# Sixteen small transfers in an earlier slot, one issuing queue, low parts on GpSimd, and three batches in another order

## The chip, the cores and the metric

The kernel runs on one core of a Trainium2 chip. The metric is the device time of one execution in microseconds (us); lower is better. Five engines work side by side: TensorE (PE) multiplies, VectorE (DVE), ScalarE (ACT) and GpSimd (POOL) do the rest, and SyncE (SP) only issues transfers (DMAs). ACT issues some transfers too, and does nothing else while one of its issues is held back.

## The reference

Two small attentions are computed between `x` and a state of 32 vectors per head, their results are put behind one another (512 + 32 tokens for each of 8 batches, 512 wide), and a gated two-layer network is applied to all 4608 tokens.

```python
B, H, S, Ns, D = (8, 8, 512, 32, 64)
a = softmax(x @ state.T / 8);   xread = a @ state
a2 = softmax(state @ x.T / 8);  sread = a2 @ x
t = concatenate([xread, sread], axis=2).transpose(0, 2, 1, 3).reshape(B * 544, H * D)
h = t @ w_in                    # 512 x 2048
g = h * tanh(softplus(h))       # mish
out = g @ w_out                 # 2048 x 512
```

The 256 `sread` tokens are called the read vectors below.

## The kernel before

Every fp32 product is made of three products of rounded parts (hi by hi, hi by lo, lo by hi); ACT makes a high part by a cast, DVE the low part by a subtraction (`ah`/`al`, `gh`/`gl`, `swh`/`swl`, `srT`).

The work goes batch by batch. For `xread` the kernel never forms the 512 tokens: it multiplies the state by `w_in` (`swp`, needing slices of `w_in` that are loaded again from memory, `w_in_again`), and then the softmax `a` by that product (`ph`). ACT turns `ph` by Mish into a unit `u`; POOL sums parts of units (`sums`), ACT and DVE split them (`gh`, `gl`), and PE multiplies them with `w_out` and sums of it into four accumulators (`acc_one`, `acc_two`, `acc_top`, `acc_end`: seven products in place of eight). At the end of a half batch ACT and DVE add the accumulators up (`sums<-acc_one` and so on) before PE may start the next half in the same banks.

Beside it the next batches are prepared. `e2_turned` (steps `tu`, `TU`; line 392) transposes the second softmax on DVE (`u<-e`), and 16 DMAs (line 404) put the 32-row quarters in place (`e2T`), which PE multiplies with `x` into `srp`; DVE scales that to the read vectors `srds`. `soft1_a` (step `PR`) makes `ah` and `al` of the next batch.

The read vectors of all batches go through the network at the end of batch 6 and in batch 7 (`ph_s`). For this those of batches 0 to 5 are transposed on DVE (`sr_turned`) and moved by 16 DMAs on SP (`sr_moved`, line 548; step `rm`), and split into `srT` high and low parts (step `rs`); those of batches 6 and 7 are turned on PE (`srTp`, step `rt`).

The order on each engine is written out by hand: a string of steps for batch 0 (line 873 on) and a `TABLE` for batches 1 to 7 (line 1061 on), one row for each of 8 slots (a slot multiplies one 256-wide piece of `w_in`). `G`, `M` are the projection and its Mish; `A`, `B` multiply a unit with `w_out`, `P`, `p` prepare one; `wN` loads a slice of `w_in` again; `lx`, `ly` load `x`. Each engine keeps this order strictly (class `InOrder`), so an instruction that waits holds all that follows it there. The DMAs of SP and ACT take eight completion semaphores in turn, and each is issued only when the transfer eight back, whichever of the two engines issued it, has landed.

Batch 7's `x` and four of its 16 `e2T` DMAs are issued by ACT:

```python
(nc.scalar if b in (1, B - 1) and 4 * q + c < 4 else nc.sync).dma_start(
    both[quad(q), c].rearrange("p k t n -> p (k t n)"), u[quad(c), q].rearrange("i k m -> i (k m)"))
```

Of the kernel before, what the change touches and what calls it, by code (L numbers as in the profile page):

```python
# [9 lines left out]
F32 = mybir.dt.float32  # L10
# [7 lines left out]
P = 128  # L18
B, H, S, NS, D = 8, 8, 512, 32, 64
# [3 lines left out]
NT = S // P  # L23
# [11 lines left out]
def as_f32(ap):  # L35
    return ap.bitcast(F32)
# [16 lines left out]
def quad(q):  # L53
    return slice(q * NS, (q + 1) * NS)
# [27 lines left out]
def state_attention_mish_kernel(ctx, tc, x, state, w_in, w_out, out):  # L82

    nc = tc.nc
    pe, dve, act, pool_e = (InOrder(tc, e) for e in (nc.tensor, nc.vector, nc.scalar, nc.gpsimd))
# [3 lines left out]
    pool = ctx.enter_context(tc.tile_pool(name="pool", bufs=2))  # L89
# [36 lines left out]
    def load_x(b, xs=None, by=nc.sync):  # L126

        shape = [P, NC, 2, NT * D]
        if xs is not None:
            pass  # L130
        elif b == 0:
            xs = const.tile(shape, F32, tag="wo7", name="x_0")
        else:
            tag, bufs = ("x", 1) if b == 2 else ("raw", 2)
            xs = pool.tile(shape, F32, tag=tag, name=f"x_{b}", bufs=bufs)
        for c in range(NC):
            last["load"] = by.dma_start(
                xs[c] if isinstance(xs, list) else xs[:, c],
                x[b].rearrange("(c k) (p t) d -> c p k (t d)", k=2, t=NT)[c])
        return xs  # L140
# [127 lines left out]
    xss = {0: load_x(0)}  # L268
# [7 lines left out]
    def attention(b, sn, x_in=None):  # L276
        sc, e2T, srd, aT = {}, {}, {}, {}
# [114 lines left out]
        def e2_turned():  # L392

            both = pool.tile([P, NC, 2, NT, NS], F32, tag="e2T", name=f"e2T_{b}", bufs=1)
            for kc in range(2):
                e2T[kc] = both[:, :, kc]
            u = pool.tile([P, 4, 2, NT * NS], F32, tag={0: "u0", 2: "sw2"}.get(b, "sc"), name=f"u_{b}", bufs=1)
            for kc in range(2):
                dve.transpose(
                    u[:, :, kc].rearrange("i q (t n) -> i t q n", t=NT),  # L400
                    e2s[kc].rearrange("n (t q p) -> n t q p", t=NT, q=4))
            for c in range(NC):
                for q in range(4):
                    (nc.scalar if b in (1, B - 1) and 4 * q + c < 4 else nc.sync).dma_start(  # L404
                        both[quad(q), c].rearrange("p k t n -> p (k t n)"), u[quad(c), q].rearrange("i k m -> i (k m)"))

        two = range(2)
# [121 lines left out]

    srds = {}  # L530

    def srT_parts(bs, c, values):
        hi, lo = (srT[c // 2][:, :, i, bs.start * NS:bs.stop * NS].rearrange("p c (b n) -> p c b n", n=NS) for i in range(2))
        act.copy(hi, values)
        dve.tensor_sub(lo, values, as_f32(hi))

    early = range(B - 2)

# [14 lines left out]
    def sreads_split():  # L553
        for c, tag in ((0, "sc"), (2, "e2T")):
            srT.append(pool.tile([P, 2, 2, B * NS], F32R, tag=tag, name=f"srT_{c}", bufs=1))
            srT_parts(early, c, srds["moved"][:, c:c + 2])

    def sread_transposed():
        pt = misc("srTp")[:, :2 * P].rearrange("p (b c n) -> p b c n", b=2, n=NS)
# [98 lines left out]
    def s_item(j, r, k):  # L658


        fc = 2 * r + k
        w = wis[B - 1, j][:, :, fc * P:(fc + 1) * P]
        if (j, r, k) == (0, 0, 1):
            both = pool.tile([P, 2, NC, P], F32R, tag="wt", name="w_0_0_1", bufs=1)
            hi, lo = both[:, 0], both[:, 1]
        else:
            hi, lo = (pool.tile([P, NC, P], F32R, tag="t", name=f"w{n}_{j}_{r}_{k}", bufs=5) for n in "hl")
        act.copy(hi, w)
        dve.tensor_sub(lo, w, as_f32(hi))
        yield  # L670
        ph = (misc, first_bank)[k](f"ph_s_{j}_{r}_{k}")
        for c in range(NC):
            pe.matmul(
                ph, hi[:, c], srT[c // 2][:, c % 2].rearrange("p i t -> p (i t)"), start=(c == 0), stop=(c == NC - 1))
        for c in range(NC):
            pe.matmul(
                ph[:, :256], lo[:, c], srT[c // 2][:, c % 2, 0], start=False, stop=(c == NC - 1), skip_group_check=True)
        yield
        unit = made["s", 0, 2 * j + r] if k else new_unit("s", 0, 2 * j + r)
        to = unit[:, 1 - k].rearrange("f h t -> f (h t)")  # L680
        act.copy(to, ph[:, 256:])
        dve.tensor_add(to, to, ph[:, :256])
        yield
        last["mish"] = act.activation(to, to, AF.Mish)
# [188 lines left out]
    for step in """  # L873
            st st st x0 x1 ldi0 x2 x3 sc hia0 ldi1 acc sc sc sc hib0 sc dia0 tr0 tr0 tr1 tr0 ldo0 tr1 jia0 cib0
            tr1 st ex0 ex1 jib0 no fill6 sw0 cib1 cia1 no coa0 ldi2 sw0 fill2 ldo1 pr0 pr0 hia1 ldi4 pr1 ldi3
            dob0 pr0 hib1 pr1 sw0 hoa0 qa0 qb0 ldo2 ldi5 jia1 jib1 di2 hob0 hi2 fill2 pr1 sw1 sw1 qb1 qa1 ji2
            ldo3 fill2 sw1 ma0 joa0 mb0 job0 ko1 ma0 mb0 wha0 sw2 p1 lx co1 loa0 sw2 la0 ci3 m1 ldo4 whb0 ga0
            lb0 sw2 lob0 ko1 ldo5 ga0 ga0 ja1 ga0 gb0 hi3 ho2 m1 ji3 gb0 gb0 lg1 ja1 gb0 p2 ci4 co2 ldo6 ldi6
            lo1 do3 sw3 g1 jo2 sw3 hi4 ji4 jo2 sw3 lo2 n2 g1 n2 X1 ho3 lg2 ldi7 g1 X2 jo3 p3 mm1 hi5 ho4 m3 sw4
            di5 g1 X3 sw4 jo3 g2 ji5 co4 sw4 g2 m3 ho5 lo3 jo4 lg3 ST X0 g2 jo4 g2 co5 hi6 di6 sw5 p4 sw5 n4 lo4  # L880
            sw5 n4 XD0 ja5 ci7 g3 g3 ja5 g3 lg4 p5 ji6 m5 g3 g4 mm0 ee0 SC SC lo5 hi7 ee1 xi2 g4 sw6 m5 g4 lg5
            ldo7 sw6 SC TR1 g4 ji7 sw7 ho6 ee0 sw6 p6 ho7 co6 ee1 TR0 g5 TR1 g5 TR0 EX1 tu EX0 ja6 sw7 n6 co7 g5
            n6 NO xz0 sw7 ja6 g5 NO PR0 xy0 next lg6 lo6 p7 PR0 PR1 g6 g6 n7 PR0 PR1 next g6 sr0 sr1 ja7 PR1 n7
            sr0 g6 sr1 next ja7 lg7 lo7
            """.split():
        what, i = re.fullmatch(r"([a-zA-Z]+)(\d*)", step).groups()
        if not hasattr(begun.get(step), "send"):
            begun[step] = steps[what](int(i or 0))
        if hasattr(begun[step], "send"):
            next(begun[step], None)  # L890

    A12, A22, A11, A21 = range(4)
    S1, S3, S2, S4 = range(3, 7)
    T3, T4, T2 = range(3)
# [57 lines left out]
    def sevens(key, p):  # L952
        return {2: FIRST, 3: FIRST + 1 + p}.get(key, SEVEN)
# [38 lines left out]

    def sums_of(key, p, banks):

        tag, bufs = ("g", 6) if (key, p) == (B - 2, 0) else ("wt", 1)
        e = banks["sums"] = pool.tile([P, 4, 256], F32, tag=tag, name=f"sums_{key}_{p}", bufs=bufs)
        one, two = (banks[n].rearrange("t (h e) -> t h e", h=2) for n in ("one", "two"))
        act.copy(e[:, 0], one[:, 0])
        dve.tensor_sub(e[:, 3], e[:, 0], one[:, 1])
        dve.tensor_add(e[:, 1:3], two, e[:, 3:].to_broadcast([P, 2, 256]))  # L1000
        if sevens(key, p) < SLOTS:
            dve.tensor_add(e[:, 3], e[:, 1], two[:, 1])
        else:
            dve.scalar_tensor_tensor(e[:, 3], e[:, 1], -1.0, two[:, 1], ALU.mult, ALU.subtract)
# [48 lines left out]
    def half_slot(key, j, at):  # L1053
# [4 lines left out]
        elif ready and (ready[0][:2] != (key, 0) or ready[0][2] < j + (j == SLOTS - 1 and at)):  # L1058
# [1 line left out]

    TABLE = {
        1: """
            G0 M0 G1 M1 mm0 mm1 ee0 ee1 A h l X0 X1 ee0 ee1 X2 X3 XD tu w0
            G0 M0 G1 M1 S2 S2 h S2 B l ST w1
            G0 M0 G1 M1 h A B l
            G0 M0 G1 M1 h A SC sr0 sr1 S4 S6 SC sr0 sr1 S4 S4 S6 S6 lx B l MM0 MM1 T0
            G0 M0 G1 M1 h T0 A TR0 TR1 w2 B l T0 TR0 TR1 T1
            G0 M0 G1 M1 EE0 EE1 EX0 EX1 T1 h A w3 B l T1 NO EE0 EE1 T2 NO
            G0 M0 G1 M1 h A PR0 PR1 B l
            G0 M0 G1 M1 h PR0 PR1 A N0 PR0 PR1 N0 N0 T2 B l li""",  # L1070
        2: """
            G0 M0 G1 M1 X0 X1 X2 X3 T2 A T3
            G0 M0 G1 M1 S2 S2 S2 T3 XD B ST T3 A T4
            G0 M0 G1 M1 T4 w4 P p B P p T4 T4 tu
            P G0 M0 p G1 M1 P p A S4 SC S4 S4 SC w5 P p B MM0 MM1""",
        3: """
            P G0 M0 p G1 M1 P p X0 X1 A P X2 X3 p B
            P G0 M0 p G1 M1 S2 P p S2 S2 XD A ST P p B
# [22 lines left out]
        B - 2: """  # L1101
            P G0 M0 p G1 M1 P p X0 X1 A P X2 X3 p B
            P G0 M0 p G1 M1 S2 P p S2 S2 XD A ST P p B
            P G0 M0 p G1 M1 P p w4 A P p B
            P G0 M0 p G1 M1 P p A S4 SC S4 S4 SC lx w5 P p B MM0 MM1
            P G0 M0 p G1 M1 rm P p TR0 TR1 A P rm TR0 TR1 p B
            P G0 M0 p G1 M1 S6 sr0 sr1 P p S6 S6 sr0 sr1 w2 ly EE0 EE1 EX0 EX1 A EE0 EE1 P p TU B NO
            P G0 M0 p G1 M1 P p NO PR0 PR1 A P p B
            P G0 M0 p G1 M1 N0 PR0 PR1 P p N0 N0 PR0 PR1 A P p SR0 SR1 SR0 SR1 w3 rs B U rt W0 A W1 P p""",
        B - 1: """  # L1110
            P G0 M0 p G1 M1 P p A P p w4 B
            P G0 M0 p G1 M1 S2 P p S2 S2 w5 A P p B
# [14 lines left out]
    for key in [*range(1, B - 1), "s", B - 1]:  # L1127
        if key == "s":
            for i, item in enumerate(items):
                j, r, k = i // 4, i // 2 % 2, i % 2  # L1130
# [29 lines left out]
            xss[b] = load_x(b)  # L1160

        def load_last():
            xss[B - 1] = load_x(B - 1, by=nc.scalar)

        def load_next():
            global_next = key + 2
# [36 lines left out]
        for j, line in enumerate(steps_of(key)):  # L1203
# [11 lines left out]
            for step in line:  # L1215
                what, i = re.fullmatch(r"([a-zA-Z]+)(\d*)", step).groups()
                name = step if what == "T" else (key, step)
# [34 lines left out]
```

## Time and profile before

| | |
|---|---|
| median of 3 runs | 648.79 us (648.32 to 651.68) |
| the profiled execution | 649.55 us, of which the span from first to last instruction is 647.7 |
| PE busy | 628.2 us, 97% of the span |
| DVE, ACT, POOL busy | 441.3, 354.6, 197.9 us |
| mean granted TensorE clock | 0.991 of full speed |

PE is idle for 647.7 - 628.2 = 19.5 us in all. Its busy time also holds stretches at a lower granted clock, in which the same matmuls take longer. In a row of a timeline the number in brackets is the time for which the engine stood idle just before it, with what ended that; "ACTq" and "SPq" rows are issues of DMAs.

### The profile page before, as it was taken

Reading aid. Unit: us, or ns where it says so; the run is one execution under the profiler, and the core shown is the slowest. Engines: PE = TensorE matmul, PEld = TensorE weight load, DVE = VectorE, ACT = ScalarE, POOL = GpSimd, SP = SyncE. Lnnn points to the kernel's source line nnn. Section 1 sums busy time; section 2 is a strip of 40 time slices with the busy share of each in tenths; the row PEclk is TensorE's granted clock in tenths of the full one; section 3 lists DMA queues with packets and bytes.
Section 4 is the critical chain, followed back from the end, with each engine's and each line's share of the span. In section 5 each row is a group of like instructions: output and inputs, shape, how many; then the busy total and the mean of one; then the engine's idle time right before and its main releaser. Section 6 shows DMA issues by size and latency. Waiting matters only on the chain.

```text
span 647.7 us, 13630 instructions
## 1 busy us (share of the span) xinstructions
PE 628.2 (97%) x5379; PEld 536.2 (83%) x5379; DVE 441.3 (68%) x757; ACT 354.6 (55%) x720; POOL 197.9 (31%) x307
## 2 busy tenths in 40 slices
PE   8999999999999999999999999999996899999997
PEld 5776777787787887888888899888885799989897
DVE  5998965548676856887697856686582876635264
ACT  4998765455455534645456644654552566544442
POOL 0000000032432232304531663256321543443274
PEclk9999999999999999999999999999998899999999
DMA  8999904701446254614454455435524324320000
GB/s 323 410 323 326 333 28 116 229 23 50 123 124 202 66 151 129 195 50 131 116 171 124 125 143 164 132 77 148 163 93 134 98 66 131 99 66 16 19 33 32
DMA packets 71711, 88.77 MB, mean 137 GB/s; under 512 B 13792, under 2 KB 48608, under 8 KB 71648
## 3 DMA queue, kind: packets, MB, share of 16 engines
q1 hardware_dynamic: 69744, 86.40, 42.6%
q10 hardware_dynamic: 1904, 1.51, 0.8%
q8 instruction: 42, 0.69, 0.5%
q14 instruction: 21, 0.17, 0.1%
HBM read 62.85 MB, written 13.11 MB: 117 GB/s over the span
## 4 chain that ended last, share of the span: by engine, by line
PE 76%; DVE 8%; DMA 7%; ACT 4%; SPq 2%; issue 1%; POOL 0%; DVEq 0%; ACTq 0%
PE ph L74 22%; PE acc_top L74 10%; PE acc L74 10%; PE acc_one L74 8%; PE acc_two L74 8%; PE acc_end L74 6%; PE swp L74 4%; DMA wir<-in_moe_w_in_dram 3%; PE ph_s L74 3%; DVE gl L74 2%; SPq L404 2%; DMA e2T<-u 1%; PE srp L74 1%; PE acc_s_one L74 1%; DMA w_in<-w_in_again 1%
## 5 line engine op out<-in xcount | busy, mean ns | idle before, releaser
L74 POOL TENSOR_TENSOR sums<-u 128x256 f32<-128x256 f32 x87 | 68.7, 789 | 249.4 <-DVE gl L74 156.7
L74 ACT ACTIVATE u<-ph 128x256 f32<-128x256 f32 x192 | 63.2, 382 | 85.1 <-PE ph L74 81.8
L74 POOL TENSOR_TENSOR sums<-sums,u 128x128 f32<-128x128 f32 x174 | 101.6, 584 | 13.7
L74 DVE TENSOR_TENSOR gl<-u,gh 128x384 fp32r<-128x384 f32 (+1 forms) x96 | 58.4, 609 | 56.1 <-ACT gh L74 55.3
L74 DVE TENSOR_TENSOR gl<-sums,gh 128x512 fp32r<-128x512 f32 x87 | 66.2, 761 | 29.5 <-ACT gh L74 29.5
L74 PE MATMUL acc<-wo,gh 128*128 128x512 f32 x256 | 80.1, 394 | 0.0
L74 PE MATMUL ph<-ah,swh 128*128 128x512 f32 (+1 forms) x228 | 71.6, 396 | 7.4 <-ACT u L74 5.9
L74 PE MATMUL acc_top<-wo,gh 128*128 128x256 f32 (+1 forms) x384 | 78.0, 295 | 0.0
L74 ACT CAST gh<-u 128x384 fp32r<-128x384 f32 x87 | 44.7, 514 | 54.7 <-PE acc_end L74 32.8
L74 PE MATMUL ph<-al,swh 128*128 128x512 f32 (+1 forms) x228 | 71.1, 393 | 0.2 <-DVE al L74 0.2
L74 PE MATMUL ph<-ah,swl 128*128 128x512 f32 (+1 forms) x228 | 71.0, 392 | 0.1
L74 ACT CAST gh<-sums 128x512 fp32r<-128x512 f32 x87 | 54.1, 621 | 25.0 <-POOL sums L74 24.7
L74 PEld LDWEIGHTS acc_top<-wo,gh 128*128 128x128 f32 x384 | 61.0, 193 | 2.7 <-issue 0.8
L74 POOL TENSOR_TENSOR w_sums<-w_sums 128x256 f32<-128x256 f32 x16 | 13.0, 812 | 155.9 <-DVE w_sums L74 147.2
L74 PEld LDWEIGHTS acc<-wo,gh 128*128 128x128 f32 x256 | 47.4, 188 | 13.0 <-issue 3.3
L74 PE MATMUL acc_top<-wo,gl 128*128 128x256 f32 (+1 forms) x192 | 56.3, 293 | 0.0
L74 DVE TENSOR_TENSOR swl<-swp,swh 128x512 fp32r<-128x512 f32 (+1 forms) x60 | 36.4, 647 | 25.3 <-ACT swh L74 25.3
L74 PEld LDWEIGHTS ph<-ah,swh 128*128 128x128 f32 x228 | 40.2, 191 | 15.5 <-ACT u L74 6.1
L74 PEld LDWEIGHTS ph<-al,swh 128*128 128x128 f32 x228 | 43.1, 190 | 10.5 <-DVE al L74 1.2
L74 PEld LDWEIGHTS ph<-ah,swl 128*128 128x128 f32 x228 | 43.2, 190 | 9.9 <-DVE swl L74 0.7
L74 PE MATMUL acc<-wo,gl 128*128 128x512 f32 x128 | 49.9, 390 | 0.0
L74 ACT CAST swh<-swp 128x512 fp32r<-128x512 f32 (+1 forms) x60 | 30.5, 562 | 23.2 <-PE swp L74 23.2
(232 smaller groups left out, 1400.3 us busy)
## 6 DMA issues: line engine op xcount, KB each, us to landing
w_in<-w_in_again SPq DMA_DIRECT2D x27, 1024.0 KB, 5.9
wir<-in_moe_w_in_dram SPq DMA_DIRECT2D x16, 512.0 KB, 10.2
wor<-in_moe_w_out_dram SPq DMA_DIRECT2D x16, 512.0 KB, 9.5
x<-in_x_dram SPq DMA_DIRECT2D x28, 256.0 KB, 4.0
x_rows<-x_turned SPq DMA_DIRECT2D x56, 128.0 KB, 2.4
x_in<-in_x_dram SPq DMA_DIRECT2D x24, 256.0 KB, 3.1
out_dram<-sums SPq DMA_DIRECT2D x23, 256.0 KB, 5.2
w_in_again<-w_in_sb SPq DMA_DIRECT2D x4, 1024.0 KB, 9.5
```

Of the source, the lines that this page charges most:

```text
L74: made = method(*args, **kwargs)
L404: (nc.scalar if b in (1, B - 1) and 4 * q + c < 4 else nc.sync).dma_start(both[quad(q), c].rearrange("p k t n -> p (k t n)"), u[quad(c), q ...
```

## The change

It has five parts. (1) In batch 6 the step `rm` (two transposes, 16 DMAs) moves from slot 4 to slot 2 (slots are counted from 0). (2) Batch 7's `x` and all its `e2T` DMAs are issued by SP, `x` ahead of the `w_in` load of step `w2`. Its `u` transposes move ahead of the preparation of a unit. (3) The low parts of `srT` of batches 0 to 5 are made by POOL. (4) In batch 6 `al` is made after the first read vectors' weights, `sums_(5,1)` takes a buffer of `g` (`sr_moved` now holds the one it had), and one `ph_s` takes another PSUM bank. (5) In batch 2 the `e2T` step moves a slot back, behind two `w_in` loads; in batch 1 the transfers and `e2T` move a slot back, behind the `sw_1_2` parts, with `u` in another buffer and `sr`, `lx` a slot later; in batch 0 the steps `hi6 di6` (which scale a piece of `w_in` as it comes in) move behind a Mish, which makes the ACT tables change twice more.

```diff
-            u = pool.tile([P, 4, 2, NT * NS], F32, tag={0: "u0", 2: "sw2"}.get(b, "sc"), name=f"u_{b}", bufs=1)
+            u = pool.tile([P, 4, 2, NT * NS], F32, tag={0: "u0", 1: "wt", 2: "sw2"}.get(b, "sc"), name=f"u_{b}", bufs=1)
...
-                    (nc.scalar if b in (1, B - 1) and 4 * q + c < 4 else nc.sync).dma_start(
+                    (nc.scalar if b == 1 and 4 * q + c < 4 else nc.sync).dma_start(
...
-    def srT_parts(bs, c, values):
+    def srT_parts(bs, c, values, by=dve):
...
-        dve.tensor_sub(lo, values, as_f32(hi))
+        by.tensor_sub(lo, values, as_f32(hi))
...
-            srT_parts(early, c, srds["moved"][:, c:c + 2])
+            srT_parts(early, c, srds["moved"][:, c:c + 2], pool_e)
...
-        ph = (misc, first_bank)[k](f"ph_s_{j}_{r}_{k}")
+        ph = (misc, misc if (j, r) == (3, 1) else first_bank)[k](f"ph_s_{j}_{r}_{k}")
...
-        tag, bufs = ("g", 6) if (key, p) == (B - 2, 0) else ("wt", 1)
+        tag, bufs = ("g", 6) if (key, p) in ((B - 3, 1), (B - 2, 0)) else ("wt", 1)
...
-            P G0 M0 p G1 M1 P p w4 A P p B
+            P G0 M0 p G1 M1 P p w4 rm A P p rm B
...
-            xss[B - 1] = load_x(B - 1, by=nc.scalar)
+            xss[B - 1] = load_x(B - 1)
```

On SP, in batch 6, this is the order of the issues before (`w_in_5508` is the load of step `w4`, `w_in_5919` that of `w2`, `x_5649` batch 6's own next `x`):

```order
L572 DMA w_in_5508<-w_in_again 128x4x512
L137 DMA x_5649<-in_x_dram 128x2x256 x4
L572 DMA w_in_5654<-w_in_again 128x4x512
L692 DMA out_dram<-sums_1_5678 128x2x256 x2
L548 DMA sr_moved<-sr_turned_5740 32x192 x8
L548 DMA sr_moved<-sr_turned_5792 32x192 x8
L572 DMA w_in_5919<-w_in_again 128x4x512
L404 DMA e2T_5971<-u_5972 32x256 x12
L572 DMA w_in_6213<-w_in_again 128x4x512
```

And this is the same stretch of SP after the change, with the same loads under new numbers:

```order
L572 DMA w_in_5508<-w_in_again 128x4x512
L548 DMA sr_moved<-sr_turned_5511 32x192 x8
L548 DMA sr_moved<-sr_turned_5552 32x192 x8
L137 DMA x_5670<-in_x_dram 128x2x256 x4
L572 DMA w_in_5675<-w_in_again 128x4x512
L692 DMA out_dram<-sums_1_5699 128x2x256 x2
L137 DMA x_5919<-in_x_dram 128x2x256 x4
L572 DMA w_in_5924<-w_in_again 128x4x512
L404 DMA e2T_5961<-u_5962 32x256 x16
L572 DMA w_in_6211<-w_in_again 128x4x512
```

The 16 `sr_moved` issues left the place between the output and the `w_in` load, and batch 7's `x` and four more `e2T` stand there or right behind.

On ACT, at the end of batch 6's slot 5 and the start of slot 6, this stood before (`u_0_6`, `u_1_6` are the two units of slot 6):

```order
L74 CAST gh_0_5_5961<-sums_0_5_5963 128x512
L137 DMA x_5921<-in_x_dram 128x2x256 x4
L404 DMA e2T_5971<-u_5972 32x256 x4
L74 ACT_TABLE_LOAD
L74 ACTIVATE u_0_6_6025<-ph_6_0_6018 128x256
L74 ACTIVATE u_1_6_6027<-ph_6_0_6018 128x256
```

And this stands there now:

```order
L74 CAST gh_0_5_5981<-sums_0_5_5983 128x512
L74 ACT_TABLE_LOAD
L74 ACTIVATE u_0_6_6025<-ph_6_0_6018 128x256
L74 ACTIVATE u_1_6_6027<-ph_6_0_6018 128x256
L74 ACTIVATE u_0_6_6025<-ph_6_1_6029 128x256
```

No issue of a DMA is left between the cast and the table load.

On DVE, at the end of the first half of batch 6's output (slot 7), this stood before (`sums_6233` adds up the accumulators of that half):

```order
L74 TENSOR_TENSOR al_6135<-at_0_6050,ah_6134 128x512
L74 TENSOR_TENSOR al_6135<-at_1_6052,ah_6134 128x512
L74 TENSOR_TENSOR gl_1_0_6169<-u_1_0_5276,gh_1_0_6168 128x384
L74 TENSOR_TENSOR gl_1_0_6169<-sums_1_0_6170,gh_1_0_6168 128x512
L74 TENSOR_SCALAR srds<-srp_6178,rs_0_5956 128x64
L74 TENSOR_SCALAR srds<-srp_6178,rs_1_5959 128x64
L74 TENSOR_TENSOR srT_6215<-sr_moved,srT_6215 128x2x192
L74 TENSOR_TENSOR srT_6218<-sr_moved,srT_6218 128x2x192
L74 TENSOR_TENSOR sums_6233<-sums_6233,acc_0_one 128x256
```

And this stands there now, down to the two `al` rows:

```order
L74 TENSOR_TENSOR gl_1_0_6167<-u_1_0_5276,gh_1_0_6166 128x384
L74 TENSOR_TENSOR gl_1_0_6167<-sums_1_0_6168,gh_1_0_6166 128x512
L74 TENSOR_SCALAR srds<-srp_6176,rs_0_5956 128x64
L74 TENSOR_SCALAR srds<-srp_6176,rs_1_5959 128x64
L74 TENSOR_TENSOR sums_6231<-sums_6231,acc_0_one 128x256
L74 TENSOR_TENSOR sums_6231<-acc_0_two,sums_6231 128x512
L74 SCALAR_TENSOR_TENSOR sums_6231<-sums_6231,acc_0_two 128x256
L74 TENSOR_TENSOR sums_6231<-acc_0_top,sums_6231 128x2x256
L74 TENSOR_TENSOR sums_6231<-acc_0_end,sums_6231 128x256
L74 TENSOR_TENSOR srT_6213<-srTp,srT_6213 128x2x64
L74 TENSOR_TENSOR srT_6216<-srTp,srT_6216 128x2x64
L74 TENSOR_TENSOR wl_0_0_6266<-w_in_5924,wh_0_0_6265 128x512
```

Four DVE instructions left the way to `sums`: two went to POOL, and the two `al` now follow behind `wl_0_0`.

## Rows read from the trace of the kernel before

**Rows 1.** Window: length, busy PE, PEld, DVE, ACT, POOL, granted clock, DMA share, GB/s
```profile
60.00:200.00 140.00, 139.03 (x1059) 109.79 (x1057) 97.09 (x155) 77.81 (x136) 27.78 (x37) 1.00 0.44 133
...
480.00:520.00 40.00, 31.61 (x272) 27.66 (x271) 22.50 (x48) 18.04 (x41) 11.32 (x18) 0.87 0.36 111
```
**Rows 2.** Waits of PE: for whom, us in total, times, longest
```profile
PE ph L74 <- ACT u L74: 5.9, 1, 5.9
PE acc_one L74 <- DVE sums L74: 1.6, 1, 1.6
...
PE ph L74 <- ACT g L74: 1.4, 1, 1.4
PE swp L74 <- DMA w_in<-w_in_again: 1.2, 1, 1.2
PE srTp L74 <- DVE srds L74: 0.9, 1, 0.9
...
PE ph L74 <- DVE sw L74: 0.5, 1, 0.5
```
**Rows 3.** Timeline of ACT: start, us, what [idle before]
```profile
487.50 7.64 ACTq L404 DMA_DIRECT2D e2T<-u  x4
495.25 1.28 ACT L74 ACT_TABLE_LOAD   x1 [11.24 <-DMA e2T<-u]
```
**Rows 4.** Timeline of SP in batch 6
```profile
461.01 1.93 SPq L137 DMA_DIRECT2D x<-in_x_dram  x4
...
473.62 11.38 SPq L548 DMA_DIRECT2D sr_moved<-sr_turned  x16
485.10 0.58 SPq L572 DMA_DIRECT2D w_in<-w_in_again  x1
486.49 12.31 SPq L404 DMA_DIRECT2D e2T<-u  x12
```
**Rows 5.** DMA issues at 485 to 486: KB each, us to landing
```profile
w_in<-w_in_again SPq DMA_DIRECT2D x1, 1024.0 KB, 8.2
```
**Rows 6.** The same view of two stretches behind stalls
```profile
496.50:502.50 6.00, 5.25 (x12) 3.80 (x12) 2.75 (x6) 2.89 (x9) 1.88 (x3) 0.50 0.12 31
...
513.50:516.50 3.00, 3.00 (x15) 3.00 (x16) 2.40 (x7) 0.96 (x3) 0.00 (x0) 0.50 0.19 67
```
**Rows 7.** Timeline of DVE: a low part in slot 2; before the second stall
```profile
454.14 0.69 DVE L74 TENSOR_TENSOR gl<-sums,gh 128x512 fp32r<-128x512 f32 x1
...
507.73 1.85 DVE L74 TENSOR_TENSOR al<-at,ah 128x512 fp32r<-128x512 f32 x2
...
511.23 1.64 DVE L74 TENSOR_TENSOR srT<-sr_moved,srT 128x384 fp32r<-128x384 f32 x2
512.78 0.41 DVE L74 TENSOR_TENSOR sums<-sums,acc_one 128x256 f32<-128x256 f32 x1
...
513.95 0.42 DVE L74 SCALAR_TENSOR_TENSOR sums<-sums,acc_two 128x256 f32<-128x256 f32 x1
```
**Rows 8.** Timeline of ACT before the second stall
```profile
509.88 0.37 ACT L74 COPY sums<-acc_one 128x256 f32<-128x256 f32 x1 [0.94 <-PE acc_end L74]
```
**Rows 9.** Timeline of PE: the last slice with `w_in` of slot 5, `srp` of batch 7
```profile
475.98 1.09 PE L74 MATMUL swp<-w_in,bd 64*32 64x256 f32 x32
...
505.43 1.10 PE L74 MATMUL srp<-x,e2T 128*32 128x64 f32 x64
```
**Rows 10.** The chain that ended last: one landing of e2T
```profile
493.56 1.70 DMA e2T<-u
```
**Rows 11.** Timeline of SP in batch 2
```profile
184.50 10.51 SPq L404 DMA_DIRECT2D e2T<-u  x16
195.11 7.68 SPq L572 DMA_DIRECT2D w_in<-w_in_again  x3
```
**Rows 12.** Timeline of PE in batch 0
```profile
88.83 1.05 PE L74 MATMUL srp<-x_again,e2T 128*32 128x64 f32 x58 [0.19 <-issue]
```
**Rows 13.** The profile's groups: one of POOL
```profile
L74 POOL TENSOR_TENSOR sums<-u 128x256 f32<-128x256 f32 x87 | 68.7, 789 | 249.4 <-DVE gl L74 156.7
```

More of the change, by code (lines that the diff above doesn't have):

```diff
@@ L879, in state_attention_mish_kernel @@
             lo1 do3 sw3 g1 jo2 sw3 hi4 ji4 jo2 sw3 lo2 n2 g1 n2 X1 ho3 lg2 ldi7 g1 X2 jo3 p3 mm1 hi5 ho4 m3 sw4
-            di5 g1 X3 sw4 jo3 g2 ji5 co4 sw4 g2 m3 ho5 lo3 jo4 lg3 ST X0 g2 jo4 g2 co5 hi6 di6 sw5 p4 sw5 n4 lo4
-            sw5 n4 XD0 ja5 ci7 g3 g3 ja5 g3 lg4 p5 ji6 m5 g3 g4 mm0 ee0 SC SC lo5 hi7 ee1 xi2 g4 sw6 m5 g4 lg5
+            di5 g1 X3 sw4 jo3 g2 ji5 co4 sw4 g2 m3 ho5 lo3 jo4 lg3 ST X0 g2 jo4 g2 co5 sw5 p4 sw5 n4 sw5 hi6 di6
+            lo4 n4 XD0 ja5 ci7 g3 g3 ja5 g3 lg4 p5 ji6 m5 g3 g4 mm0 ee0 SC SC lo5 hi7 ee1 xi2 g4 sw6 m5 g4 lg5
             ldo7 sw6 SC TR1 g4 ji7 sw7 ho6 ee0 sw6 p6 ho7 co6 ee1 TR0 g5 TR1 g5 TR0 EX1 tu EX0 ja6 sw7 n6 co7 g5
@@ L1062, in state_attention_mish_kernel @@
         1: """
-            G0 M0 G1 M1 mm0 mm1 ee0 ee1 A h l X0 X1 ee0 ee1 X2 X3 XD tu w0
-            G0 M0 G1 M1 S2 S2 h S2 B l ST w1
+            G0 M0 G1 M1 mm0 mm1 ee0 ee1 A h l X0 X1 ee0 ee1
+            G0 M0 G1 M1 S2 S2 h S2 X2 X3 XD tu w0 B l ST w1
             G0 M0 G1 M1 h A B l
-            G0 M0 G1 M1 h A SC sr0 sr1 S4 S6 SC sr0 sr1 S4 S4 S6 S6 lx B l MM0 MM1 T0
-            G0 M0 G1 M1 h T0 A TR0 TR1 w2 B l T0 TR0 TR1 T1
+            G0 M0 G1 M1 h A SC S4 S6 SC S4 S4 S6 S6 B l MM0 MM1 T0
+            G0 M0 G1 M1 h sr0 sr1 T0 A sr0 sr1 TR0 TR1 lx w2 B l T0 TR0 TR1 T1
             G0 M0 G1 M1 EE0 EE1 EX0 EX1 T1 h A w3 B l T1 NO EE0 EE1 T2 NO
@@ L1073, in state_attention_mish_kernel @@
             G0 M0 G1 M1 S2 S2 S2 T3 XD B ST T3 A T4
-            G0 M0 G1 M1 T4 w4 P p B P p T4 T4 tu
-            P G0 M0 p G1 M1 P p A S4 SC S4 S4 SC w5 P p B MM0 MM1""",
+            G0 M0 G1 M1 T4 w4 P p B P p T4 T4
+            P G0 M0 p G1 M1 P p A S4 SC S4 S4 SC w5 P p tu B MM0 MM1""",
         3: """
@@ L1103, in state_attention_mish_kernel @@
             P G0 M0 p G1 M1 S2 P p S2 S2 XD A ST P p B
-            P G0 M0 p G1 M1 P p w4 A P p B
+            P G0 M0 p G1 M1 P p w4 rm A P p rm B
             P G0 M0 p G1 M1 P p A S4 SC S4 S4 SC lx w5 P p B MM0 MM1
-            P G0 M0 p G1 M1 rm P p TR0 TR1 A P rm TR0 TR1 p B
-            P G0 M0 p G1 M1 S6 sr0 sr1 P p S6 S6 sr0 sr1 w2 ly EE0 EE1 EX0 EX1 A EE0 EE1 P p TU B NO
+            P G0 M0 p G1 M1 P p TR0 TR1 A P TR0 TR1 p B
+            P G0 M0 p G1 M1 S6 sr0 sr1 P p S6 S6 sr0 sr1 ly w2 EE0 EE1 EX0 EX1 A EE0 EE1 TU P p B NO
             P G0 M0 p G1 M1 P p NO PR0 PR1 A P p B
-            P G0 M0 p G1 M1 N0 PR0 PR1 P p N0 N0 PR0 PR1 A P p SR0 SR1 SR0 SR1 w3 rs B U rt W0 A W1 P p""",
+            P G0 M0 p G1 M1 N0 PR0 PR1 P p N0 N0 A P p SR0 SR1 SR0 SR1 w3 rs B U rt W0 A PR0 PR1 W1 P p""",
         B - 1: """
```

## The prediction

> **What bounds the kernel now.** I read the busy shares first. TensorE (PE) is busy for 628.2 of 647.7 us, so whatever another engine saves is worth nothing unless PE stands idle for it, or runs at a lower clock because of it. Next I cut the span into windows, and one stands out: between 480 and 520 us PE is busy for 31.61 of 40 us, at a granted clock of 0.87 [rows 1]. So the place to look at is the end of batch 6.
>
> The list of PE's waits names who is late [rows 2]. One wait of 5.9 us is for ACT's units, at 497 us. Two more follow near 511 to 513 us: 0.9 for `srds` and 1.6 for `sums`, both DVE's. Elsewhere there are 1.4 (ACT `g`, batch 0), 1.2 (a `w_in` load, batch 2) and 0.5 (DVE `sw`, batch 1).
>
> Why is ACT late at 497? Its timeline shows four `e2T` issues that take 7.64 us from 487.50 on, and only then the table load that the Mish needs, after 11.24 us without work [rows 3]. Four free issues would take about 2.6 us (10.51 us for 16, so 0.66 each [rows 11]). What holds them is seen on SP: 16 `sr_moved` issues fill 473.62 to 485.00, the 1 MB `w_in` load goes out behind them at 485.10 [rows 4], and takes 8.2 us to land [rows 5], which is 493.3. The issues on ACT and SP take eight semaphores in turn, so they come to a stop until that load is in. The chain therefore runs: `sr_moved` late, `w_in` late, ACT's issues held, Mish late, PE idle.
>
> Each long stall costs twice, since PE comes back at the lower of its two clock levels (1.2 GHz, granted 0.50). Behind the first it is busy for 5.25 us at 0.50, behind the second for 3.00 us [rows 6]. At full clock these matmuls would take half of that.
>
> **The change, part by part.** The sum is made against the profiled execution, 649.55 us; the median, 648.79, is 0.76 lower.
>
> *The first stall.* With `sr_moved` gone from SP and no DMA issue left on ACT there, the table load follows ACT's last cast directly. PE's wait for the units goes: **5.9** us [rows 2]. The half clock behind it: 5.25/2 = **2.6** [rows 6]. Bounds: nothing, if ACT finds another late thing there, to 8.5.
>
> Does something else come late instead? All 16 `e2T` now stand on SP behind batch 7's `x` and the `w_in` load. `x` takes the buffer that the last slice of slot 5 leaves at 475.98 + 1.09 = 477.1 [rows 9]. Two slots earlier the same pair, 4 x `x` and a `w_in`, went out from 461.01, the `w_in` at 461.01 + 1.93 = 462.9 [rows 4]; with 8.2 us to landing [rows 5] that is 10.1 us for the pair. So `w_in` lands at about 487.2, 6 us sooner than before. The first seven `e2T` can go before it; nine are left, 9 x 0.66 = 5.9, and the last takes 1.70 to land [rows 10]: about 494.8. PE needs it at `srp`, at 505.43 before [rows 9], now 5.9 + 2.6 sooner: 496.9. The margin is 2.1 us. It is the thinnest of this forecast and gives the first rival.
>
> The other side of the move: `sr_moved` now stands ahead of batch 6's next `x` and `w_in`. Its second transpose follows a DVE low part that ended at 454.83 [rows 7]. Eight issues from there, with some still to go of the first eight, end near 462 (16 x 0.66 from 451.5), so `x` goes out about 1 us later than at 461.01, and the `w_in` lands near 472.2. PE takes it at 475.98 [rows 9]. Free, with 3.8 us to spare; beyond that every us of delay would stall PE.
>
> *The second stall.* On DVE, `al` (1.85) and two low parts of `srT` (1.64) stood ahead of `sums` [rows 7]. With both gone `srds` comes 1.85 sooner: the 0.9 goes. `sums` needs ACT's copy, which ends at 509.88 + 0.37 = 510.25 [rows 8], so DVE starts it there and not at 512.78. PE, which without waits is there 2.5 us before 513.25, at 510.75, followed the start by 0.47: 510.72, no wait. The second accumulator is free once two more sums are read out of it, before at 513.95 + 0.42 = 514.37, 1.6 after the first began [rows 7], so now at 511.85, where PE wants it at about 511.5. I leave 0.3 to 0.75 as still waited for and take 0.75: 2.5 - 0.75 = **1.75**. A gap this short leaves the clock up, I take it: the 1.2 of [rows 2] stands in a window whose clock is 1.00 [rows 1]; so 3.00/2 = **1.5** [rows 6] comes back too. Bounds 0 to 4.0.
>
> What is put in their place: the two `al` now stand between the weights of the first and the second `ph_s`, so the second one's low part comes up to 1.85 later. Part of that is covered by the first `ph_s`; between 0 and 1.85 I take the middle, **-0.95**.
>
> The two low parts on POOL: the nearest row is 0.789 us for 256 columns [rows 13], so 384 take 1.18, two 2.4; DVE took 0.82 each. They stand between two POOL sums of the half batch, several us before the first `ph_s` reads them. Nothing, and up to 2.4 if that cover is gone.
>
> *Batch 2.* Sixteen `e2T` issues (184.50 to 195.01) stood ahead of three `w_in` loads [rows 11]. Two loads now go first: **1.2** [rows 2], and `e2T` 2 x 0.66 and a slot's work later, still ahead of its `srp` at 204.8. Bounds 0 to 1.2, less if `e2T` is late.
>
> *Batch 1.* The `sw` parts now precede the `x_turned` transposes: **0.5** [rows 2].
>
> *Batch 0.* The Mish `g` no longer waits behind the scaling of `w_in`, so 1.4 of waiting goes [rows 2]; but at 88.83 `srp` starts as soon as its `e2T` lands [rows 12], and that chain hangs on transfers, not on PE, so what PE gains ahead is waited for there: **0**. Two more table loads of 1.28 [rows 3] lie on ACT, off PE's path: 0, at most -2.6. Bounds -2.6 to +1.4.
>
> The buffer of `g` and the PSUM bank only change which release is waited for, and none of PE's waits names one: 0.
>
> Sum: 5.9 + 2.6 + 1.75 + 1.5 - 0.95 + 1.2 + 0.5 + 0 = 12.5. 649.55 - 12.5 = 637.05 for a profiled execution; less 0.76, **636.3 us** as median.
>
> A rule that speaks against it: the Trainium skill (DMA: Bandwidth & Descriptors, "Issuing engines are not separate DMA queues") says that DMAs issued by different engines end on the same 16 DMA engines, so that a second issuer saves only sequencer time, which is usually small. By that, taking four issues off ACT is worth their sequencer time, an estimate of 2.6 us, and the data come no sooner. The trace differs in the size: the four took 7.64 us, because the issuer was held for a load.
>
> **Rivals.**
> 1. *The first stall moves to `e2T`.* The transfers land as late as they ever did and only the engine that suffers is another: `srp` waits. If SP is held twice by `x` and `w_in`, the last `e2T` lands 2 us after PE wants it, PE then comes back at the lower clock and loses about 2.6 again: 636.3 + 4.6 = 640.9. For it: the issues of SP took 12.31 us for 12 when a load was in the way [rows 4]. Against: the load is 6 us earlier. 0.14.
> 2. *The second stall stays.* ACT's copy of `acc_one` waits for something that my view does not show (0.94 <- PE `acc_end` [rows 8], with PE's matmuls of `acc_one` long over), and `sums` is no earlier: +1.75 + 1.5, so 639.6. 0.12.
> 3. *The batch 0 tables are on the path:* +2.6, 638.9. 0.06.
> 4. *ACT is not freed.* Units of slots 4 and 5 wait for the buffers that `sr_turned` now holds, while its transfers wait in SP's queue, and the Mish of an earlier slot is late by as much as was gained: nothing changes, 647 to 650. Against: the transfers are to land by 464, a slot before. 0.05.
> 5. *Slower: DVE waits for a buffer in slot 2.* The two `sr_turned` take unit buffers two slots earlier, when the units of batch 5 still hold some. If the first is held, DVE stands, and with it every `gl` behind it and PE. A hold of t costs PE nearly t, and 2.6 for the half clock behind it: from t = 10 on the 12.5 are gone, and at 13.5 the kernel takes 652. Against: at that place the transpose follows the low part of one of the oldest units, whose buffer is then free. 0.03.
>
> **How the numbers follow.** Forecast 0.60, then 0.14, 0.12, 0.06, 0.05, 0.03. The forecast's own range is 634.0 (no `al` cost, some of batch 0's 1.4) to 638.2 (`al` full, more of the second stall). A range of 634.0 to 641.2 takes in the first three rivals; 0.08 and the tails stay out. A measurement of this kernel tells some 0.5%, 3.2 us, from no change: faster 0.92, within 0.5% 0.05, slower 0.03.
>
> **What would show it.** In the profile after: no ACT wait for `e2T`, and no PE wait for ACT `u` of several us; granted clock 1.00 from 480 to 500; PE busy over 39 of 40 us in that window; `sums` no more than 0.75 behind; the last `e2T` landing before `srp` asks. It is wrong if `srp` shows a wait for a DMA, if a `swp` of batch 6 waits for `w_in`, or if a new wait for ACT `g` stands in batch 0.

## The result, and the profile after

The changed kernel takes 634.70 us (median of 6 executions, 634.36 to 637.16) against 649.56 for the kernel before (6 executions). The ratio is 0.9777, with a 95% interval of 0.9755 to 0.9799; by the ratio that is 14.5 us, and the medians are 14.9 apart. The forecast was 636.3. The profiled execution took 634.78 us, its span is 633.0 against 647.7, so the two traces differ by 14.7 us.

The busy times and the two windows that answer to [rows 1]:

```profile
PE 624.3 (99%) x5379; PEld 533.5 (84%) x5379; DVE 440.7 (70%) x755; ACT 357.2 (56%) x722; POOL 199.3 (31%) x309
```

```profile
60.00:200.00 140.00, 138.70 (x1086) 109.14 (x1085) 96.10 (x156) 77.98 (x138) 27.46 (x37) 1.00 0.45 138
...
480.00:520.00 40.00, 39.31 (x350) 35.11 (x350) 29.21 (x54) 23.69 (x55) 19.60 (x29) 1.00 0.33 105
```

In the second PE is now busy for 39.31 us, at a granted clock of 1.00. Of the six waits of PE in [rows 2] five are gone, and the one of `acc_one` has shrunk from 1.6 us to 0.2:

```profile
PE srp L74 <- DMA e2T<-u: 0.9, 1, 0.9
...
PE acc_two L74 <- DVE sums L74: 0.3, 1, 0.3
...
PE acc_one L74 <- DVE sums L74: 0.2, 1, 0.2
PE ph_s L74 <- DVE w L74: 0.2, 1, 0.2
```

The wait of 0.9 for `e2T` is one of batch 0, not of batch 7. On ACT's timeline, against [rows 3], the table load has come forward from 495.25, and what it waited for is gone:

```profile
480.55 1.28 ACT L74 ACT_TABLE_LOAD   x1
482.25 0.66 ACT L74 ACTIVATE u<-ph 128x256 f32<-128x256 f32 x2 [0.42 <-PE ph L74]
```

SP's timeline, against [rows 4]: the 16 moves stand in slot 2, and the `e2T` issues run without a hold, 10.44 us for 16.

```profile
449.27 10.63 SPq L548 DMA_DIRECT2D sr_moved<-sr_turned  x16
460.00 2.07 SPq L137 DMA_DIRECT2D x<-in_x_dram  x4
462.17 0.59 SPq L572 DMA_DIRECT2D w_in<-w_in_again  x1
...
474.69 1.92 SPq L137 DMA_DIRECT2D x<-in_x_dram  x4
476.72 0.58 SPq L572 DMA_DIRECT2D w_in<-w_in_again  x1
480.18 10.44 SPq L404 DMA_DIRECT2D e2T<-u  x16
```

To see where the 14.7 us came from, four points of PE's timeline are set side by side: `srp` of batch 2, those of batches 6 and 7 (both computed during batch 6, two slots apart), and the first `ph_s`. Before:

```profile
204.79 1.10 PE L74 MATMUL srp<-x,e2T 128*32 128x64 f32 x64
...
477.23 1.10 PE L74 MATMUL srp<-x,e2T 128*32 128x64 f32 x64 [0.16 <-ACT u L74]
...
517.34 1.08 PE L74 MATMUL ph_s<-srT,wh 128*128 128x512 f32 x4
```

and after:

```profile
202.05 1.10 PE L74 MATMUL srp<-x,e2T 128*32 128x64 f32 x64
...
474.49 1.10 PE L74 MATMUL srp<-x,e2T 128*32 128x64 f32 x64
...
493.93 1.10 PE L74 MATMUL srp<-x,e2T 128*32 128x64 f32 x64
...
502.43 1.18 PE L74 MATMUL ph_s<-srT,wh 128*128 128x512 f32 x4
```

With `srp` of batch 7 at 505.43 before [rows 9], each stretch can be compared with its term of the sum:

| stretch | before | after | gained | forecast |
|---|---|---|---|---|
| start to `srp` of batch 2 (batches 0 to 2) | 204.79 | 202.05 | 2.74 | 1.2 + 0.5 + 0 = 1.7 |
| to `srp` of batch 6 | 272.44 | 272.44 | 0 | 0 |
| to `srp` of batch 7 (first stall) | 28.20 | 19.44 | 8.76 | 5.9 + 2.6 = 8.5 |
| to the first `ph_s` (second stall) | 11.91 | 8.50 | 3.41 | 1.75 + 1.5 = 3.25 |
| to the end (`al` behind `ph_s`) | 130.36 | 130.57 | -0.21 | -0.95 |
| span | 647.7 | 633.0 | 14.7 | 12.5 |

### The profile page after: what moved, and what is told of

Read it like the earlier page. It is cut to its first block, busy times and chain, and to the rows that moved or that the text cites. A ratio compares the mean times of both kernels' runs of the same rounds, so it can differ in the third digit from the quotient of the medians.

```text
span 633.0 us, 13643 instructions
## 1 busy us (share of the span) xinstructions
PE 624.3 (99%) x5379; PEld 533.5 (84%) x5379; DVE 440.7 (70%) x755; ACT 357.2 (56%) x722; POOL 199.3 (31%) x309
## 4 chain that ended last, share of the span: by engine, by line
PE 82%; DMA 4%; DVE 3%; ACT 1%; SPq 1%; issue 1%; DVEq 0%
PE ph L74 24%; PE acc_top L74 11%; PE acc_one L74 10%; PE acc_two L74 9%; PE acc L74 8%; PE acc_end L74 6%; PE swp L74 4%; PE ph_s L74 3%; PE srp L74 1%; DMA w_in_again<-w_in_sb 1%; DMA x_again<-in_x_dram 1%; PE acc_s_one L74 1%; PE acc_s_top L74 1%; PE acc_s_two L74 1%; DMA out_dram<-sums 1%
```

## The experiments

The theory: three separate things were on PE's path, worth 8.5, 3.3 and some 2 us. The first is the place of the 16 moves on SP, which made the `w_in` load late, which held ACT's issues. Rivals are told with each experiment. Places in time are those of the kernel's own profile.

**Only the moves go forward.** The kernel before, with `rm` in slot 2, and with the buffer for `sums_(5,1)` that this needs:

```diff
-            P G0 M0 p G1 M1 P p w4 A P p B
+            P G0 M0 p G1 M1 P p w4 rm A P p rm B
...
-            P G0 M0 p G1 M1 rm P p TR0 TR1 A P rm TR0 TR1 p B
+            P G0 M0 p G1 M1 P p TR0 TR1 A P TR0 TR1 p B
```

> The kernel before with one thing changed: the 16 moves of the read vectors go in slot 2 (with the buffer for sums that this needs). ACT still issues batch 7's x and four e2T, and al and the low parts stand where they stood. Theory (the moves alone made the first stall; issues on ACT are held only to about 486, before PE wants the units): the wait of 5.9 and the 2.6 of half clock go, the second stall stays: 641.0 against 649.5. Rival (the issues on ACT carry part of it): a wait of PE for u of 2 us or more stays, 643 to 645.

Measured: 640.41 us, ratio 0.9883 (0.9860 to 0.9906). The stretch from `srp` of batch 6 to that of batch 7 is 19.44 us, to the hundredth that of the changed kernel, and ACT's four issues are not held (PE's timeline, then ACT's):

```profile
476.37 1.10 PE L74 MATMUL srp<-x,e2T 128*32 128x64 f32 x64
...
495.81 1.10 PE L74 MATMUL srp<-x,e2T 128*32 128x64 f32 x64
```

```profile
484.38 2.46 ACTq L404 DMA_DIRECT2D e2T<-u  x4
```

PE has no wait for `u` left, and both waits of the second stall are still there (1.6 and 0.9 us before):

```profile
PE acc_one L74 <- DVE sums L74: 1.6, 1, 1.6
...
PE srTp L74 <- DVE srds L74: 1.1, 1, 1.1
```

So the moves alone give the whole of the first term. With the moves early, who issues `e2T` has no part in it.

**The moves stay late, SP issues all.** The changed kernel with the two lines of the table put back:

> The changed kernel with the 16 moves of the read vectors back in slot 4; batch 7's x and e2T stay on SP. Theory (what held everything is the w_in load and the transfers behind the 16 moves): ACT is free, but w_in lands at about 492, the last e2T near 500, and srp waits for it some 6 us, then 2.6 of half clock: about 643. Rival (only the four issues on ACT were the trouble): srp waits under 1 us, 634.7 to 636.

Measured: 642.08 us, ratio 0.9894 (0.9863 to 0.9925), 7.4 above the changed kernel. ACT was free (its table load came at 481.15), and PE now waits for the transfers themselves, in three pieces of 4.0 us, and comes back at the lower clock. Timeline of PE, then the window behind it:

```profile
494.31 0.27 PE L74 MATMUL srp<-x,e2T 128*32 128x64 f32 x2 [0.23 <-DMA e2T<-u]
496.24 0.27 PE L74 MATMUL srp<-x,e2T 128*32 128x64 f32 x2 [1.66 <-DMA e2T<-u]
498.67 1.88 PE L74 MATMUL srp<-x,e2T 128*32 128x64 f32 x58 [2.15 <-DMA e2T<-u]
```

```profile
498.00:504.00 6.00, 5.33 (x74) 5.19 (x75) 0.48 (x2) 1.02 (x2) 3.67 (x6) 0.50 0.30 88
```

5.33/2 = 2.7 for the clock, and 4.0 of waits: 6.7 of the 7.4. This is the prediction's first rival made real: with the moves late, freeing ACT only hands the stall to `srp`.

**The moves are early, ACT issues again.** The changed kernel with this, and with `w2` ahead of `ly` and `TU` behind the unit as before:

```diff
-                    (nc.scalar if b == 1 and 4 * q + c < 4 else nc.sync).dma_start(
+                    (nc.scalar if b in (1, B - 1) and 4 * q + c < 4 else nc.sync).dma_start(
...
-            xss[B - 1] = load_x(B - 1)
+            xss[B - 1] = load_x(B - 1, by=nc.scalar)
```

> The changed kernel with batch 7's x and four e2T back on ACT, w_in first on SP, u transposed late again; the 16 moves stay in slot 2. Theory (an issue is held until the w_in load of slot 5 has landed, now near 483): ACT's four issues end near 484.5 and the table load follows, 4 us later than in the changed kernel; PE waits 2 to 3 us for u: 637 to 640. Rival (with the moves gone nothing holds the issues, four cost their 2.6 us of ACT): 634.7 to 635.5, no wait of PE for u over 0.5.

Measured: 635.55 us (633.91 to 636.53), ratio 0.9789 (0.9757 to 0.9822), not to be told from the changed kernel's. My theory's number fell; the rival's held within the noise, and so did its sign, no wait of PE for `u`. ACT's timeline:

```profile
483.60 2.46 ACTq L404 DMA_DIRECT2D e2T<-u  x4
486.08 1.28 ACT L74 ACT_TABLE_LOAD   x1 [4.46 <-DMA e2T<-u]
487.38 1.21 ACT L74 ACTIVATE u<-ph 128x256 f32<-128x256 f32 x4
```

The four issues took 2.46 us: nothing held them, since `w_in`, issued at 475.78 with 5.7 us to landing, was in at 481.5. The table load is 5.5 us later than in the changed kernel all the same (1.1 of it because this execution was that much later already at `srp` of batch 6), because the transposes came late, and still PE has no wait for `u`: it asks for the freed banks only with the next slot's first product, at 489.54, and the units were done at 488.59. I had left this slack out when I put 2 to 3 us on the delay.

**Only the second stall.** The kernel before, with the low parts on POOL and `al` behind the first weights:

```diff
-            P G0 M0 p G1 M1 N0 PR0 PR1 P p N0 N0 PR0 PR1 A P p SR0 SR1 SR0 SR1 w3 rs B U rt W0 A W1 P p""",
+            P G0 M0 p G1 M1 N0 PR0 PR1 P p N0 N0 A P p SR0 SR1 SR0 SR1 w3 rs B U rt W0 A PR0 PR1 W1 P p""",
...
-            srT_parts(early, c, srds["moved"][:, c:c + 2])
+            srT_parts(early, c, srds["moved"][:, c:c + 2], pool_e)
```

> The kernel before with only the second stall's parts changed: low parts of srT on GpSimd, al behind the first weights of ph_s. Theory (the stalls are separate and each worth what its rows say): waits for srds and sums fall from 2.5 to 0.5 or 0.8 and the half clock there (1.5) goes: 645.8 to 646.5 against 649.5; the first stall is as it was. Rival (the clock there is not up, since the first stall is 14 us earlier): 647.5.

Measured: 645.60 us, ratio 0.9961 (0.9942 to 0.9980). The first stall is untouched (PE waits 6.0 for `u`), and from `srp` of batch 7 to `ph_s` it is 8.51 us against 11.91 before and 8.50 in the changed kernel. In the profiles the two stalls are separate. PE's timeline, then the windows of these 8.5 us, at clock 1.00:

```profile
504.31 1.10 PE L74 MATMUL srp<-x,e2T 128*32 128x64 f32 x64
...
512.82 1.17 PE L74 MATMUL ph_s<-srT,wh 128*128 128x512 f32 x4
```

```profile
503.00:508.00 5.00, 5.00 (x98) 4.78 (x97) 3.84 (x7) 4.33 (x9) 3.57 (x6) 1.00 0.20 50
508.00:513.00 5.00, 4.49 (x35) 4.02 (x34) 3.47 (x10) 1.70 (x5) 4.69 (x8) 1.00 0.62 211
```

This kernel, in which ACT issues, and the earlier one in which the moves stay late and SP issues all have the late moves and the changed second stall in common. From `srp` of batch 6 to the first `ph_s` this one takes 36.49 us (476.33 to 512.82), the earlier one 35.21 (474.35 to 509.56). So with the moves late, part (2) of the change is worth some 1.3 of the 8.8 us, by one execution of each.

**Each half of it undone, and both.** Three kernels: the changed one with the low parts back on DVE, with `al` back where it was, and with both (the lines of the last diff, turned round).

Low parts on DVE: 

> The changed kernel with the two low parts of srT for batches 0 to 5 back on DVE, ahead of sums. Theory (sums can begin at 498.78, when ACT's copy is done; two low parts of 0.82 behind srds push it to about 499.5): PE's wait for sums grows from 0.5 to 1.2 us, too short a gap for the clock: 635.4. Rival (any longer gap there brings the half clock back): 637.

`al` early: 

> The changed kernel with al made early again, ahead of gl of the second half. Theory: al takes 1.6 to 1.85 of DVE, srds and sums come up to 1.0 us later than ACT's copy allows; PE waits 0.5 to 1.0 more for srds and sums, and 0.2 less at ph_s; clock stays up: 635.4. Rival (half clock behind the gap): 637.

Both: 

> The changed kernel with the low parts on DVE and al early. Theory: the second stall is back as it was, 0.9 for srds and 1.6 for sums against 0.5, and with two gaps so close the half clock too (1.5): 634.7 + 2.0 + 1.5 = 638.2. Rival (the clock fell there only as a remnant of the first stall 12 us earlier, which is gone): 636.7, granted clock 1.00 throughout.

Measured: 635.83 us, 0.9803 (0.9779 to 0.9828); 636.74, 0.9813 (0.9790 to 0.9837); 637.70, 0.9821 (0.9796 to 0.9847). The order is the expected one, but each interval overlaps that of the changed kernel, so the medians do not show what a half is worth. In the profiles the second stall of the last kernel is back whole: 12.07 us from `srp` to `ph_s`, waits of 1.1 and 1.6, and PE busy for all of 502 to 505 us at a granted clock of 0.50. With the first stall gone, the clock there was no remnant of it, so that rival falls.

The gaps of the first two were 1.6 and 1.8 us, larger than expected, and the clock behind them went two ways. With the low parts on DVE it fell (the timeline of PE, then a window):

```profile
499.45 0.50 PE L74 MATMUL acc_one<-wo,gh 128*128 128x256 f32 x2 [1.56 <-DVE sums L74]
```

```profile
501.00:504.00 3.00, 3.00 (x16) 3.00 (x15) 2.44 (x7) 2.26 (x6) 0.00 (x0) 0.51 0.52 175
```

With `al` early, behind the longer gap, it did not:

```profile
499.50 0.33 PE L74 MATMUL srTp<-ident,srds 128*128 128x128 f32 x1 [1.82 <-DVE srds L74]
```

```profile
499.00:504.00 5.00, 4.20 (x26) 3.61 (x27) 4.37 (x12) 2.14 (x6) 3.16 (x6) 1.00 0.32 108
```

That is one execution of each. So the clock fell behind the shorter gap and not behind the longer, and neither my "clock stays up" nor its rival is right for both. Of the five executions of the second kernel this one has a mean clock of 0.999 and takes 634.80; the other four have 0.997 and take 636.52 to 638.57. The clock may have fallen behind the same gap there, but this is not shown: they have no trace, and the changed kernel, whose profile has only waits of 0.2 and 0.3 us at this place, has an execution with 0.997 and 637.16 us too.

**Only the first batches.** The kernel before with the new order of batches 0 to 2:

> The kernel before with the new order of batches 0 to 2 alone; the end of batch 6 is untouched. Theory (the waits of batches 0 to 2 stand on the path and are worth 1.2 + 0.5 + 1.2 = 2.9 us): about 646.6 us against 649.5, and both long stalls of batch 6 as before (5.9, and 0.9 + 1.6). Rival (what PE gains early is waited for at a transfer later): 649.5.

Measured: 647.45 us, ratio 0.9976 (0.9958 to 0.9995), so 0.3 to 2.7 us faster; `srp` of batch 2 stands at 202.16, and the waits for `w_in`, `sw` and `g` are gone. The theory's 2.9 lies just outside the interval, the rival's 0 outside it too; the prediction's 1.7 lies inside.

The three kernels with one part each gain 1.6 (this one), 7.6 (the moves) and 2.5 us (the second stall) by their ratios, 11.7 together, against 14.5 for the whole change. Each of these figures is uncertain by more than 1 us, so the difference can be noise; that the parts add up is read from the stretches of the profiles, not from the medians.

**Batch 0 put back.** The changed kernel with the string of batch 0 as before (`hi6 di6` ahead of the Mish again):

> The changed kernel with batch 0 in its old order. Theory (batch 0's Mish wait was worth 1.2, as srp starts 1.2 sooner in the changed kernel): 635.9, the wait of 1.4 for g back, srp at 88.8. Rival (the earlier e2T of batch 0 comes from elsewhere, as I predicted in giving this part 0): 634.7.

Measured: 634.72 us, ratio 0.9780 (0.9757 to 0.9802), equal to the changed kernel. The wait for `g` is back, and the one for `e2T` is gone:

```profile
PE ph L74 <- ACT g L74: 1.4, 1, 1.4
```

The rival holds. Here PE reaches batch 0's `srp` at 87.91 and finds `e2T` there; in the changed kernel it came at 86.41 and was held until 87.59. What PE gains ahead of this `srp` it waits for there, for the most part. `srp` of batch 2 is at 202.59.

**The hold made in another place.** The changed kernel with four of batch 0's `e2T` on ACT:

```diff
-                    (nc.scalar if b == 1 and 4 * q + c < 4 else nc.sync).dma_start(
+                    (nc.scalar if b < 2 and 4 * q + c < 4 else nc.sync).dma_start(
```

> The changed kernel with four of batch 0's sixteen e2T issued by ACT, as batch 1 has it. Theory (an engine that issues is held by the transfer eight back; here a 1 MB store of w_in_again goes out just ahead): ACT stands some 6 to 8 us from 74 on, PE waits for its units and comes back at the lower clock: 638 to 645. Rival (a second issuer saves sequencer time): SP's 16 issues become 12, the last e2T lands 2.6 us sooner and the wait of 0.9 us for it goes: 633.8.

Measured: 639.33 us, ratio 0.9851 (0.9819 to 0.9883), 4.6 slower than the changed kernel. ACT's timeline, and the window in which PE pays for it:

```profile
80.88 0.52 ACTq L404 DMA_DIRECT2D e2T<-u  x1
81.44 0.60 ACT L74 ACTIVATE g<-ph 128x512 f32<-128x512 f32 x1 [2.99 <-DMA w_in_again<-w_in_sb]
```

```profile
85.00:90.00 5.00, 4.05 (x10) 3.00 (x11) 4.32 (x6) 4.40 (x8) 0.00 (x0) 0.66 0.07 20
```

The fourth issue is held until the 1 MB store that left SP ahead of it is in (issued at 73.37, 7.5 us to landing), and the Mish behind it stands for 2.99 us. PE then waits 0.6 and 1.0 us for `wo` and runs at the lower clock for a while. The theory's number held, but the hold of ACT is less than half of its 6 to 8 us. Nothing came of the 12 issues left on SP: `srp` of batch 0 has no wait, but PE reached it only at 92.11, against 87.59. The hold that is gone from batch 6 has so been made in another place, by a large transfer just ahead.

**The store moved instead.** Two kernels with the stores to `w_in_again` issued behind batch 0's `e2T`, all four, or only the last:

```diff
-                    (nc.scalar if b == 1 and 4 * q + c < 4 else nc.sync).dma_start(
+                    last["e2T", b] = (nc.scalar if b == 1 and 4 * q + c < 4 else nc.sync).dma_start(
...
-                    nc.sync.dma_start(w_in_again[:, :, g * G:(g + 1) * G], w_in_sb[:, :, g * G:(g + 1) * G])
+                    with tc.issue_after(getattr(last["e2T", 0], "ins", last["e2T", 0])):
+                        nc.sync.dma_start(w_in_again[:, :, g * G:(g + 1) * G], w_in_sb[:, :, g * G:(g + 1) * G])
```

All four: 

> The changed kernel with all four stores to w_in_again issued behind batch 0's sixteen e2T. Theory (a 1 MB store holds the e2T issues of batch 0, and the stores take transfer time in a stretch where the transfers are busy 0.99): the wait of 0.9 us for e2T goes and up to 1 us more in the first 60 us: 632.8 to 633.8. Rival (the stores then delay x_rows and e2T of batch 1, or the first loads from w_in_again): 634.7 or more, with a wait of PE for a DMA between 90 and 180.

The last alone: 

> The changed kernel with only the last of the four stores to w_in_again issued behind batch 0's sixteen e2T. Theory: e2T's issues run at 0.66 from 73.3, the last lands near 85.6, srp wants it at 86.4: the wait of 0.9 us goes, 633.8. Rival (the issues are slow for another reason, transfers that were begun before): srp still waits 0.5 or more, 634.5.

Measured: 633.38 us, ratio 0.9767 (0.9740 to 0.9794), and 634.44 us, 0.9775 (0.9749 to 0.9801). In both `srp` of batch 0 has no wait left, and its sixteen issues run without a hold, in 10.06 and 10.42 us against 12.92 in the changed kernel. In the first PE asks at 86.51, as in the changed kernel, so there the wait is really gone; in the second it asks only at 88.23, after waits of 1.4 us for `x_rows` near 64 us, so its missing wait shows less. The second kernel's time is its rival's 634.5, without the wait that the rival named; the first kernel's lies within its theory's. The first has the lowest median of all the kernels here, with a span of 631.6 us, but its interval covers the changed kernel's: that it is faster is not shown.

## Why the prediction was right

**The first stall.** Forecast 8.5, measured 8.76. The chain was right in its first link and too long in its second: the moves alone free everything, as shown by the kernel with nothing else changed. The prediction gave the gain to `sr_moved` gone from SP and to no DMA issue left on ACT; the second of these is worth nothing that can be measured once the first is done (the kernel with ACT's issues back). Without the first it is worth some 1.3 us and hands the rest of the stall to `srp`.

A rule of the Trainium skill was weighed there (DMA: Bandwidth & Descriptors, "Issuing engines are not separate DMA queues"): a second issuer saves only sequencer time. With the early moves the trace agrees, four issues took ACT 2.46 us. With four issues of batch 0 on ACT it does not: the Mish behind them came 2.99 us late for a store's landing. The Trainium skill's rule covers the issue, not the hold.

**The thin margin.** It was put at 2.1 us. The last `e2T` was issued at 490.0, and the last two took 2.9 us to land (their median), not 1.70, so as an estimate it was in at about 492.9, and PE asked at 493.93. It held, at half the size.

**The second stall.** 3.25 forecast, 3.41 measured. `srds` has no wait, `sums` began at 498.78 behind ACT's copy as worked out, and 0.5 us of waits are left where 0.75 was taken.

**`al` behind the weights.** This term was mis-sized: 0.95 taken, 0.2 measured against the kernel before, and 0.6 against the kernel that differs from the changed one only in `al` (129.99 us from the first `ph_s` to the end, against 130.57). DVE's timeline shows both `al` in 1.55 us, and the low part of the second weights right behind them:

```profile
498.78 0.42 DVE L74 TENSOR_TENSOR sums<-sums,acc_one 128x256 f32<-128x256 f32 x1 [0.90 <-ACT sums L74]
...
502.97 1.55 DVE L74 TENSOR_TENSOR al<-at,ah 128x512 fp32r<-128x512 f32 x2
504.45 0.68 DVE L74 TENSOR_TENSOR w<-w_in,w 128x512 fp32r<-128x512 f32 x1
```

PE's wait for `w` is 0.17 us, as the first `ph_s` covered most of it. The middle of the bounds was too far from nothing.

**Batches 0 to 2.** 1.7 forecast, 2.74 in this pair of profiles. The pair overstates it. Among the kernels whose first three batches are the old ones, `srp` of batch 2 stands at 204.79, 204.62 and 203.63; among the seven whose first three batches are those of the changed kernel, itself included, between 201.15 and 203.62, on average 202.1. The means differ by 2.3, with batch 0 back by 1.8. This fits 1.7 from batches 1 and 2; batch 0, which I put at 0, gave some 0.5 by these profiles and nothing in the medians. With one execution of each kernel, the split is an estimate: in the same seven, batch 0's `srp` starts anywhere from 86.12 to 89.06, before batches 1 and 2 play any part.

The prediction called itself wrong if `srp` shows a wait for a DMA. One does, 0.9 us in batch 0. It is not batch 7's, for which the sentence was written, and the part on batch 0 said that PE would wait there for what it gained ahead.

Of the rivals, the table loads of batch 0 stayed off the path, no unit buffer held DVE or ACT, and the pair of `x` and `w_in` behind the moves was issued at 460.00, in time.

What the pair of profiles gave beyond the forecast, 14.7 against 12.5, is `al` (0.74), the batches 0 to 2 (1.04) and 0.42 that the two stalls gave beyond their terms. That 636.3 lies nearer to the median than this is luck: 0.76 was taken off because the profiled execution lay so far above the median of three, and with six executions the median of the kernel before is 649.56, where there is nothing to take off.

## What to carry to other kernels

When an engine that computes also issues DMAs, look at what each issue may be held by: here a small transfer on ACT stood behind a 1 MB load or store of another queue, and the stall showed as PE waiting for ACT. Look first for the transfers that push that large one late and that nothing needs soon; moving those alone gave the whole gain of the first stall. Moving the issue to another engine gave nothing measurable on top of that, and some 1.3 of 8.8 us without it. A delay off the path has slack, so follow it to the first row that PE waits for before putting a price on it.

## What was not expected of the hardware

VectorE's low parts are slower beside POOL's two subtractions. In the kernel with `al` early, POOL made the low parts from 495.98 on, in 2.54 us, and DVE's two `gl` at that time took 1.37 and 1.48 us:

```profile
495.98 2.54 POOL L74 TENSOR_TENSOR srT<-sr_moved,srT 128x384 fp32r<-128x384 f32 x2 [1.15 <-ACT srT L74]
```

```profile
496.30 1.37 DVE L74 TENSOR_TENSOR gl<-u,gh 128x384 fp32r<-128x384 f32 x1
497.59 1.48 DVE L74 TENSOR_TENSOR gl<-sums,gh 128x512 fp32r<-128x512 f32 x1
```

In the changed kernel the same two, begun ahead of POOL's subtractions, took 0.54 and 0.68. The kernel with both halves back differs from the one with `al` early only in that DVE makes the low parts, and there they took 0.81 and 0.68. So, by one execution of each, it is POOL's subtractions that made them slow; what the two engines share is not shown. It also accounts for the gap with `al` early, 1.8 us and not 1.0.

In the changed kernel DVE stands for 0.90 us of POOL's 2.10, waiting for ACT's copy. What it does run beside the rest, `srds` and the first `sums`, took 0.47 and 0.42 us, against 0.46 and 0.41 before: these two, which read a result of PE, were not slowed. So the move cost nothing there.

The other thing is the clock: behind a gap of 1.56 us it fell in one kernel, and behind one of 1.82 us in another it did not. What decides that stays open.
